# Attention's values in plain float32, a head in each half of the array's columns, one key block for two query blocks

## The chip, the cores and the metric

The kernel runs on one core of one Trainium2 chip. The metric is the device time of one execution in microseconds (us): 2129.85 us before the change, the median of 3 runs (2129.79 to 2129.86).

## The reference

First attention: 4 batches, 8 heads, 768 tokens, head size 64, all in float32. A token sees the 4 first tokens of its sequence (the sinks) and the window of 128 tokens that ends in itself:

```
scores = scale * np.matmul(q, k.transpose(0, 1, 3, 2))
keep = is_sink | in_window            # rel >= 0 and rel < window; sinks: pos < 4
a = np.exp(scores - max) ; a = a / (a.sum(-1) + 1e-9)
attn_out = np.matmul(a, v)            # "the values"
```

The result, as 3072 rows of 512, goes through a mixture of 8 experts: gate logits `x @ w_gate`, eight rounds of row and column normalization over all tokens (Sinkhorn), and for each expert `relu(x @ w1[e]) @ w2[e]`, weighted and summed.

## The kernel before, in words

Tokens come in 24 blocks of 128 (b, i): 4 batches of 6. A *unit* n is a block with one half of the heads (hh, four heads in two pairs pr): 48 units. Each query block needs two key blocks, its own and the one before, and the 4 sinks.

A round n works on several units at once, in an order written out by hand (`early_round` for n below 6, where TensorE's order alone is fixed; `steady_round` from 6 on, where every engine's is). On TensorE (PE), steady round n issues:

- `scores(n+1)`, L463: for each pair of heads three products of the split q and k (float32r: high x high, high x low, low x high). A head's 64 rows lie in one half of the array's rows, and the two heads alternate. Head h writes the PSUM bank st*h*, one buffer each.
- `values(n-1, 0)`, L539: the first pair. V (`split_v`, L455, on POOL) and the probabilities PT (`transpose_p`, L501: ACT copies the high part L514, DVE subtracts for the low part L517) are split likewise. The stationary operand is 128 keys x the 128 columns of *two* heads, the moving one the probabilities of both heads (256 columns), so each product has two useful quarters of four. Two key blocks x three terms, and one matmul of 96 rows for the sinks: seven per pair, L555.
- one step of `run_fill` (expert 0's products, L633 and L649, spread over the rounds), a `gate_step` (L580, one matmul of the gate's logits).
- `transpose_qk(n+2)` into st0: four transposes L439; ACT casts the high part (L445), DVE subtracts the low one (L448).
- `transpose_p(n)`, pair 0 into st1, pair 1 into st2: eight transposes L510 (four where i is 0).
- `values(n-1, 1)`, the second pair, and `store_x(n-1)` (L557): ACT and DVE copy 64 rows each of O into xr (L565); SP stores xr when both halves of the heads are there, and the gate's matmuls of this block are queued for the next round.
- `transpose_sinks(n)` (L535), another gate step, another fill step.

DVE's order in the round is: `soften(n+1)` (L487, mask and minimum; ACT takes the exponentials, L490), copies that were left over, `divide(n+1)` (L496, L497; POOL scales by the reciprocal, L499), the expert fill's low part, then L448, L517 twice, L565. SP's queue loads k, q and v rows (L429) two to four rounds ahead. So `scores` of the next round waits for L448 (st0), for L517 twice (st1, st2) and for ACT's copy of the sinks' transpose (st3).

O and the gate's output share two PSUM buffers; all eight banks are taken. After attention come the Sinkhorn rounds, and experts 1 to 7 and the other two thirds of the tokens, from L904 on, which the diff leaves alone.

Of the kernel before, what the change touches and what calls it, by code (L numbers as in the profile page):

```python
# [9 lines left out]
F32 = mybir.dt.float32  # L10
# [223 lines left out]
def tile_sink_attention_moe(ctx: ExitStack, tc: tile.TileContext, q, k, v, wg, w1, w2, out):  # L234
# [60 lines left out]
    NK = H * SINK  # L295
    SK = 3 * NK
    bd = attc.tile([SK, H], F32, name="bd")
    nc.gpsimd.memset(bd, 1.0)
    for r0 in range(0, SK, NK):
        blk = bd[r0:r0 + NK, :]  # L300
        nc.gpsimd.affine_select(out=blk, in_=blk, pattern=[[-SINK, H]], compare_op=ALU.is_ge, fill=0.0,
                                base=0, channel_multiplier=1)
        last_const = nc.gpsimd.affine_select(out=blk, in_=blk, pattern=[[SINK, H]], compare_op=ALU.is_ge, fill=0.0,
                                             base=SINK - 1, channel_multiplier=-1).ins
# [68 lines left out]
    SS = []  # L373
    for j in range(2):
        s = att1.tile([P, SK], F32R, name=f"SS{j}")
        nc.vector.tensor_copy(s, zero[:, 0:SK])
        SS.append(s)
# [10 lines left out]

    units = [(b, i, hh) for b in range(B) for i in range(NB) for hh in range(2)]
# [5 lines left out]
    VSr, VSm = {}, {}  # L395
# [8 lines left out]
    def load_sinks(b):  # L404
        vs = VSr[b] = att.tile([SK, D], F32, name="vs")
        for r0 in range(0, SK, NK):
            (nc.sync if b else nc.scalar).dma_start(vs[r0:r0 + NK, :], v[b, :, 0:SINK, :])

    def spread_sinks(b):

        vm = VSm[b] = att1.tile([P, H, D], F32, name="vm")[0:SK]
        nc.gpsimd.tensor_tensor(vm, VSr[b].unsqueeze(1).broadcast_to([SK, H, D]), bd.unsqueeze(2).broadcast_to([SK, H, D]), op=ALU.mult)

    def split_sinks(b):

        VS = seq[b] = att.tile([SK, H * D], F32R, name="VS")
        vmf = VSm[b].rearrange("p h d -> p (h d)")
        nc.gpsimd.tensor_scalar(VS, vmf, 1.0, 1.0, op0=ALU.mult, op1=ALU.mult)
        nc.gpsimd.tensor_sub(VS[2 * NK:], vmf[2 * NK:], f32(VS[2 * NK:]))

    def load_rows(names, j):
        b, i = divmod(j, NB)
        cuts = (0, HH, H) if j == 0 else (0, H)
        ts = [(att.tile([P, H, D], F32, name=nm), {"kr": k, "qr": q, "vr": v}[nm]) for nm in names]
# [29 lines left out]

    def split_v(n):  # L455
        b, i, hh = units[n]
        V = att.tile([P, 2, HH * D], F32R, name="V", bufs=5)
        vs = raws["vr", b, i][:, hh * HH:(hh + 1) * HH, :].rearrange("p h d -> p (h d)")
        nc.gpsimd.tensor_scalar(V[:, 0], vs, 1.0, 1.0, op0=ALU.mult, op1=ALU.mult)
        nc.gpsimd.tensor_sub(V[:, 1], vs, f32(V[:, 0]))  # L460
        us[n]["V"] = V
# [38 lines left out]

    def transpose_p(n, pr):  # L501
# [6 lines left out]
        for j, w in enumerate(ws):  # L508
# [4 lines left out]
        PT = u["PT", pr] = att.tile([P, 2, len(ws), 2, P], F32R, name="PT", bufs=4)  # L513
        hi = nc.scalar.copy(PT[:, 0], t).ins  # L514

        def low():
            u["split"] = hi, nc.vector.tensor_sub(PT[:, 1], t, f32(PT[:, 0])).ins  # L517

        return low

    def gather_sinks(n):

        hh = units[n][2]
        ss = SS[hh]
        nk = HH * SINK
        snk = us[n]["sc"][:, :, 0:SINK]
        v3 = lambda c0: ss[:, c0 + hh * nk:c0 + (hh + 1) * nk].rearrange("p (h s) -> p h s", s=SINK)
        for c0 in (0, 2 * NK):
            nc.gpsimd.tensor_scalar(v3(c0), snk, 1.0, 1.0, op0=ALU.mult, op1=ALU.mult)
        nc.gpsimd.tensor_sub(v3(NK), snk, f32(v3(0)))  # L530

    def transpose_sinks(n):

        tsk = st_tile([SK, P], 3)
        nc.tensor.transpose(tsk, f32(SS[units[n][2]]), ident)  # L535
        PS = us[n]["PS"] = att.tile([SK, P], F32R, name="PS")
        nc.scalar.copy(PS, tsk)

    def values(n, pr):  # L539

        b, i, hh = units[n]
        u = us[n]
        if pr == 0:
            u["O"] = ps_o.tile([P, NP, 2, P], F32, name="O")
        cs = slice(pr * P, (pr + 1) * P)
        ops = []
        ws = (1,) if i == 0 else (0, 1)
        for j, w in enumerate(ws):
            V = us[n - 2 + 2 * w]["V"]
            for x_, y_ in ((0, 0), (0, 1), (1, 0)):  # L550
                ops.append((V[:, x_, cs], u["PT", pr][:, y_, j]))
        if i:
            ops.append((seq[b][:, hh * HH * D:][:, cs], u["PS"].unsqueeze(1).broadcast_to([SK, 2, P])))
        for j, (x_, y_) in enumerate(ops):
            nc.tensor.matmul(u["O"][:, pr], lhsT=x_, rhs=y_, start=(j == 0), stop=(j == len(ops) - 1))  # L555

    def store_x(n):  # L557
        b, i, hh = units[n]
        u = us[n]
        O = u["O"]  # L560
        quads = [(slice(r * D, (r + 1) * D), O[r * D:(r + 1) * D, :, r, :]) for r in range(2)]
        tok = b * S + i * P
        xr = u["xr"] = us[n - 1]["xr"] if hh else att.tile([P, KC, P], F32, name="xr")
        for (rows, o), cp_ in zip(quads, (nc.scalar.copy, nc.vector.tensor_copy)):
            cp_(xr[rows, hh * NP:(hh + 1) * NP, :], o)  # L565
        if hh == 1:
            nc.sync.dma_start(xscr[:, :, tok:tok + P].rearrange("k p t -> p k t"), xr)
            if tok < NPART:
                cols = slice(tok % HT, tok % HT + P)
                for kh in range(2):  # L570
                    x_ = xr[:, kh * KH:(kh + 1) * KH, :]
                    b_ = xblock(kh, tok // HT)
                    act_soon(lambda b_=b_, x_=x_: nc.scalar.copy(b_[:, 0, :, cols], x_))
                    pool_soon(lambda b_=b_, x_=x_: nc.gpsimd.tensor_sub(b_[:, 1, :, cols], x_, f32(b_[:, 0, :, cols])))
            later.append(gate_tile(tok // P, xr))
# [166 lines left out]
    def spin(k_, w):  # L742

        for _ in range(k_):
            nc.tensor.matmul(spare[0:SK, 0:w * SK], lhsT=SS[1], rhs=SS[1].unsqueeze(1).broadcast_to([P, w, SK]), start=True, stop=True)

    def early_round(n):

        if units[n + 2][2] == 0:
            with (tc.high_priority() if n == -2 else nullcontext()):  # L750
                load_rows(("kr", "qr"), n // 2 + 1)
                load_rows(("vr",), n // 2 + 1)
            if units[n + 2][1] == 0:
                load_sinks(units[n + 2][0])
        if n == -2:
            nc.sync.dma_start(wg_raw, wg.rearrange("(k p) e -> p k e", p=P))
            spread_sinks(0)
            split_sinks(0)
# [16 lines left out]
        if on(n - 1):  # L775
            values(n - 1, 0)
# [5 lines left out]
        if on(n):  # L782
            transpose_p(n, 0)()
            if units[n][1]:
                gather_sinks(n)
            with tc.issue_after(us[n - 1]["scaled"] if n else last_const):
                split_v(n)
# [3 lines left out]
        if on(n - 1):  # L791
            values(n - 1, 1)
            store_x(n - 1)
# [11 lines left out]
    def steady_round(n):  # L805

        if n % 2 == 0:
            if on(n + 2):
                load_rows(("vr",), n // 2 + 1)
# [13 lines left out]
        if on(n):  # L823
            if units[n][1]:
                gather_sinks(n)
            split_v(n)
# [3 lines left out]
        if on(n - 1):  # L830
            values(n - 1, 0)
# [15 lines left out]
        if on(n - 1):  # L847
            values(n - 1, 1)
# [13 lines left out]
        if on(n):  # L862
            b, i, hh = units[n]
            if (i, hh) == (0, 0):
                spread_sinks(b)
            elif (i, hh) == (0, 1):
                split_sinks(b)
# [785 lines left out]
```

## Time and profile before

| | |
|---|---|
| median of 3 runs | 2129.85 us |
| span of the profiled execution | 2128.0 us, first to last instruction |
| PE busy | 2115.4 us, 99% |
| DVE, ACT, POOL busy | 1521.0, 882.5, 751.2 us |
| attention with its fill | the rounds up to some 287 us |

Of the profiled execution the span alone is given; 1.85 us are between it and the median. Rows of the trace give an instruction's start and duration in us, its engine (PE matmul, PEld weight load, DVE, ACT, POOL, SP's queue SPq), its line, what it writes and reads, partitions x elements and a count of merged neighbours. In brackets stands how long its engine had been idle and what released it. PE's durations run from issue to the end of the result, so neighbours overlap; the distance of their starts is what each costs.

### The profile page before, as it was taken

The numbers are of one execution on the slowest core, as the hardware profiler recorded it, in microseconds if no ns is written. First come the engines' busy times: TensorE is split into PE (matmuls) and PEld (weight loads), VectorE is DVE, ScalarE is ACT, GpSimd is POOL, SyncE is SP. The second block draws the span as 40 slices with busy tenths as digits, with TensorE's granted clock in tenths as the row PEclk, the third lists the DMA queues.
The fourth block names the chain that finished last, engine by engine and source line by source line (L and its number), as shares of the span: only waits on it lengthen the run. The fifth ranks groups of instructions, "written<-read, shape, count | busy, mean of one in ns | idle before, by whom it ended". The sixth has DMA issues, their size and how long they took to land.

```text
span 2128.0 us, 31779 instructions
## 1 busy us (share of the span) xinstructions
PE 2115.4 (99%) x10541; PEld 1767.1 (83%) x10541; DVE 1521.0 (71%) x2722; ACT 882.5 (41%) x1867; POOL 751.2 (35%) x950
## 2 busy tenths in 40 slices
PE   9999999999999999999999999999999999999998
PEld 7898887888888888888888888888888888888887
DVE  8877778778777876866766666666756766666666
ACT  7877745444444443442233322332333232332322
POOL 7766642323233231232222322223322322233223
PEclk9999999999999999999999999999999999999999
DMA  6543428999999887686666666667866666666662
GB/s 146 130 101 86 96 95 271 319 295 312 294 302 305 293 290 241 226 280 199 207 195 201 207 189 207 202 203 277 282 201 192 203 204 198 200 204 195 202 198 85
DMA packets 397642, 453.83 MB, mean 213 GB/s; under 512 B 99680, under 2 KB 265760, under 8 KB 396576
## 3 DMA queue, kind: packets, MB, share of 16 engines
q1 hardware_dynamic: 397080, 451.57, 68.0%
q8 instruction: 87, 1.43, 0.3%
q14 instruction: 83, 0.68, 0.1%
q10 hardware_dynamic: 392, 0.16, 0.0%
HBM read 314.17 MB, written 137.46 MB: 212 GB/s over the span
## 4 chain that ended last, share of the span: by engine, by line
PE 95%; DVE 2%; ACT 2%; issue 0%; POOL 0%; DMA 0%; SPq 0%; DVEq 0%; POOLq 0%; ACTq 0%
PE c L916 41%; PE o L1477 20%; PE held L1477 8%; PE o L1160 7%; PE held L1160 7%; PE O L555 3%; PE st L479 2%; PE st L510 1%; PE o L649 1%; ACT sc L490 1%; PE g L633 1%; PE st L439 1%; PE st L633 0%; PE O L580 0%; DVE PT L517 0%; PE O L649 0%
## 5 line engine op out<-in xcount | busy, mean ns | idle before, releaser
L942 ACT CAST hf<-w 128x512 fp32r<-128x512 f32 x448 | 265.2, 620 | 563.9 <-POOL w L1442 299.7
L1477 PE MATMUL o<-hf,W2q 128*128 128x512 f32 x1920 | 472.0, 389 | 0.0
L1477 PEld LDWEIGHTS o<-hf,W2q 128*128 128x128 f32 x1920 | 360.1, 188 | 75.4 <-DVE acc L1491 0.9
L916 PE MATMUL c<-T,W1q 128*128 128x512 f32 x1530 | 388.9, 389 | 0.2 <-DVE w L1423 0.2
L943 DVE TENSOR_TENSOR hf<-w,hf 128x512 fp32r<-128x512 f32 x448 | 330.5, 766 | 74.8 <-ACT hf L942 67.3
L916 PEld LDWEIGHTS c<-T,W1q 128*128 128x128 f32 x1530 | 286.9, 188 | 60.6 <-DVE w L1423 0.9
L1491 DVE TENSOR_TENSOR acc<-o,acc 128x512 f32<-128x512 f32 x298 | 204.6, 687 | 170.2 <-PE o L1477 170.2
L916 PE MATMUL c<-B,W1q 128*128 128x512 f32 x1134 | 278.3, 389 | 0.0
L1442 POOL TENSOR_TENSOR w<-w 128x512 f32<-128x512 f32 x64 | 82.7, 1292 | 492.4 <-DVE w L1424 486.2
L916 PEld LDWEIGHTS c<-B,W1q 128*128 128x128 f32 x1134 | 212.6, 188 | 43.9
L1423 DVE TENSOR_TENSOR w<-c,M 128x512 f32<-128x512 f32 x192 | 132.3, 689 | 137.5 <-PE c L916 133.1
L1419 ACT COPY M<-c 128x512 f32<-128x512 f32 x192 | 112.7, 587 | 247.7 <-PE c L916 247.6
L1477 PE MATMUL held<-hf,W2q 128*128 128x512 f32 x768 | 194.8, 389 | 0.0
L916 PE MATMUL c<-T,W1f 128*128 128x512 f32 x672 | 171.1, 390 | 0.1
L1160 PE MATMUL held<-W2f,h 128*128 128x512 f32 x672 | 171.1, 390 | 0.0
L1160 PE MATMUL o<-W2f,h 128*128 128x512 f32 x672 | 170.6, 389 | 0.1
L1477 PEld LDWEIGHTS held<-hf,W2q 128*128 128x128 f32 x768 | 144.0, 188 | 29.8
L1459 POOL TENSOR_TENSOR w<-w 128x512 f32<-128x512 f32 x64 | 105.6, 1651 | 176.2 <-DVE hf L943 176.2
L1160 PEld LDWEIGHTS o<-W2f,h 128*128 128x128 f32 x672 | 126.0, 188 | 27.0 <-DVE acc L1167 0.9
L916 PEld LDWEIGHTS c<-T,W1f 128*128 128x128 f32 x672 | 125.8, 188 | 26.9 <-issue 0.5
L1160 PEld LDWEIGHTS held<-W2f,h 128*128 128x128 f32 x672 | 125.8, 188 | 26.4 <-DVE W2f L943 0.5
L969 POOL TENSOR_TENSOR r<-r 128x256 f32<-128x256 f32 x27 | 20.1, 743 | 357.7 <-ACT M L1123 221.2
(212 smaller groups left out, 3088.5 us busy)
## 6 DMA issues: line engine op xcount, KB each, us to landing
W2q<-w2s SPq DMA_DIRECT2D x448, 256.0 KB, 3.0
W1q<-w1s SPq DMA_DIRECT2D x444, 256.0 KB, 2.9
w1s<-W1f SPq DMA_DIRECT2D x56, 896.0 KB, 7.8
w2s<-WT SPq DMA_DIRECT2D x136, 256.0 KB, 3.5
r<-in_moe_w_dram SPq DMA_DIRECT2D x64, 512.0 KB, 4.4
w2s<-W2f SPq DMA_DIRECT2D x56, 256.0 KB, 4.7
PB<-psd SPq DMA_DIRECT2D x16, 512.0 KB, 4.2
w2s<-W2f SPq DMA_DIRECT2D x56, 128.0 KB, 6.5
```

The source lines that it names most:

```text
L479: nc.tensor.matmul(ps[h], lhsT=Q[r0:r0 + D, a, pr, :], rhs=K[r0:r0 + D, c, pr, :], start=(j == 0), stop=(j == 2))
L555: nc.tensor.matmul(u["O"][:, pr], lhsT=x_, rhs=y_, start=(j == 0), stop=(j == len(ops) - 1))
L916: nc.tensor.matmul(ps, lhsT=w1(a, k), rhs=x[:, b, k, :], start=(start and j == 0), stop=(stop and j == len(TERMS) - 1), skip_group_check=n ...
L942: nc.scalar.copy(dst[:, 0], src)
L943: at(1, lambda: nc.vector.tensor_sub(dst[:, 1], src, f32(dst[:, 0])))
L1160: nc.tensor.matmul(o, lhsT=h[c, th][:, a, off:off + P], rhs=W2F[n][:, w, c, :], start=(begin and c == 0 and j == 0), stop=(end and c == 1 ...
L1419: nc.scalar.copy(t, T["c2"])
L1423: nc.vector.tensor_add(w, T["c1"], T[m])
L1442: nc.gpsimd.tensor_sub(S3, T["A11"], T["A21"])
L1459: at(k, lambda: nc.gpsimd.tensor_sub(T["A11"], w, T["A11"]))
L1477: nc.tensor.matmul(o, lhsT=W2Q[part, n, m][:, a, k * P:(k + 1) * P], rhs=F[part, n, H_OF[m]][:, w, :], start=(j == 0 and (begin or not hol ...
L1491: nc.vector.tensor_add(sums[m, k], o, sums[m, k])
```

## The change

The values use V and the probabilities as they are, in plain float32. The stationary operand is one head's 64 columns of V, and its output the half of PSUM's partitions that belongs to it, so two heads sit in the two halves of the array's columns. A key block meets both query blocks that need it (its own and the next) in one matmul of 256 columns, once the next block's probabilities are there: a block's result is begun in one unit (ACT's copy to xr) and completed two units later (DVE adds), and then stored and gated. A few blocks finish at once (`whole`: blocks 1 and 3 of the first batch and the last one); blocks 2 and 4 of the first batch begin with one query. The sinks' matmul is one per head, 128 columns, with operands padded with zeros to 128 rows. `values` of both pairs now stand together behind the scores. Probabilities are kept in a ring of three places per key block; the splits of V, of the probabilities and of the sinks go. The scores, the experts and the rest are unchanged. The diff, cut to its core:

```diff
-        vm = VSm[b] = att1.tile([P, H, D], F32, name="vm")[0:SK]
-        nc.gpsimd.tensor_tensor(vm, VSr[b]..., bd..., op=ALU.mult)
-    def split_sinks(b): ...
+VSs = [att1.tile([P, 2, HH, D], F32, name=f"VS{j}") for j in range(2)]
+PSs = [att1.tile([P, P], F32, name=f"PS{j}") for j in range(4)]
+for t in VSs + PSs:
+    nc.gpsimd.memset(t, 0.0)
+    def spread_sinks(b, hh):
+        nc.gpsimd.tensor_tensor(seq[b][0:NK, hh], VSr[b][:, hh]..., bd..., op=ALU.mult)
 ...
-    def split_v(n):
-        nc.gpsimd.tensor_scalar(V[:, 0], vs, 1.0, 1.0, op0=ALU.mult, op1=ALU.mult)
-        nc.gpsimd.tensor_sub(V[:, 1], vs, f32(V[:, 0]))
 ...
+    RING = 3
+    spot = lambda n, s: (2 * block(n) + s) % RING
     def transpose_p(n, pr):
-        ws = (1,) if i == 0 else (0, 1)
+        ws = sorted([(spot(n, 0), 1)] + ([(spot(n - 2, 1), 0)] if i else []))
         t = st_tile([P, len(ws), 2, P], (2 if n < 2 else 1) + pr)
 ...
-        hi = nc.scalar.copy(PT[:, 0], t).ins
         def low():
-            u["split"] = hi, nc.vector.tensor_sub(PT[:, 1], t, f32(PT[:, 0])).ins
+            u["split"] = nc.vector.tensor_copy(PT, t).ins,
 ...
+    def due_keys(n):
+        whole = (b, i) in ((0, 1), (0, 3)) or n >= L - 2
+        if i == 0:
+            return ([(n - 2, {n - 2: 0})], [n - 2], []) if b else ([], [], [])
+        if (b, i) in ((0, 2), (0, 4)):
+            return [(n - 2, {n: 1})], [], [n]
+        return [(n - 2, {n - 2: 0, n: 1})] + ([(n, {n: 0})] if whole else []), [n - 2, n] if whole else [n - 2], [] if whole else [n]
 
     def values(n, pr):
-            for x_, y_ in ((0, 0), (0, 1), (1, 0)):
-                ops.append((V[:, x_, cs], u["PT", pr][:, y_, j]))
-            ops.append((seq[b][:, hh * HH * D:][:, cs], u["PS"].unsqueeze(1).broadcast_to([SK, 2, P])))
-            nc.tensor.matmul(u["O"][:, pr], lhsT=x_, rhs=y_, start=(j == 0), stop=(j == len(ops) - 1))
+        for m, qs in keys:
+            R = spots(PTR[hh][pr], [spot(m, s_) for s_ in qs.values()])
+            for h in range(2):
+                ops.append((h, raws[("vr", *units[m][:2])][:, hh * HH + 2 * pr + h, :], R[:, h], ...))
+        for q_ in ready:
+            if units[q_][1]:
+                for h in range(2):
+                    ops.append((h, seq[units[q_][0]][:, hh, 2 * pr + h, :], us[q_]["PS"].unsqueeze(1), ...))
+        for j, (h, x_, y_, sides) in enumerate(ops):
+            nc.tensor.matmul(u["O"][h * D:(h + 1) * D, pr, sides], lhsT=x_, rhs=y_, start=(j < 2), stop=(j >= len(ops) - 2))
 
     def store_x(n):
-        for (rows, o), cp_ in zip(quads, (nc.scalar.copy, nc.vector.tensor_copy)):
-            cp_(xr[rows, hh * NP:(hh + 1) * NP, :], o)
+        for q_ in sorted(begun + ready, key=...):
+            if "begun" in us[q_]:
+                nc.vector.tensor_add(xr[:, half, :], O, xr[:, half, :])
+            else:
+                nc.scalar.copy(xrs[block(q_)][:, half, :], O)
+        if hh == 1:
+            for q_ in ready:
+                put_x(q_)        # the store, the pieces for the experts, the gate: as before
 ...
     def steady_round(n):
-            if on(n + 2):
-                load_rows(("vr",), n // 2 + 1)
+            if on(n):
+                load_rows(("vr",), n // 2)
 ...
         if on(n - 1):
-            values(n - 1, 0)
+            for pr in range(NP):
+                values(n - 1, pr)
         run_fill(1)
 ...
         if on(n - 1):
-            values(n - 1, 1)
             store_x(n - 1)
```

The early rounds have the values together at the first place, too. The sinks of a unit are now gathered with one POOL copy instead of three operations, and their transpose has 16 columns instead of 96.

## Rows read from the trace of the kernel before

**Rows 1.** The page of the profiled execution: its span; the engines' busy time, share and instructions; PE's busy tenths and granted clock in 40 equal slices; the chain that ended last, by engine.

```profile
span 2128.0 us, 31779 instructions
...
PE 2115.4 (99%) x10541; PEld 1767.1 (83%) x10541; DVE 1521.0 (71%) x2722; ACT 882.5 (41%) x1867; POOL 751.2 (35%) x950
...
PE   9999999999999999999999999999999999999998
...
PEclk9999999999999999999999999999999999999999
...
PE 95%; DVE 2%; ACT 2%; issue 0%; POOL 0%; DMA 0%; SPq 0%; DVEq 0%; POOLq 0%; ACTq 0%
```

**Rows 2.** Busy time of each engine by stretch: us from the span's start, then the length, then busy us and instructions of PE, PEld, DVE, ACT, POOL, the granted clock, DMA share and GB/s.

```profile
34.00:287.00 253.00, 251.57 (x2176) 227.93 (x2177) 197.19 (x663) 195.98 (x608) 168.15 (x392) 1.00 0.41 96
...
340.00:2128.00 1788.00, 1780.66 (x7878) 1471.70 (x7876) 1252.13 (x1864) 642.61 (x1146) 536.09 (x464) 1.00 0.73 232
```

**Rows 3.** PE's instructions in order of time, one round (start us, duration us, engine, line, op, out<-in, stationary rows*columns, moving rows x columns, count); the first row is the start of the scores two rounds earlier.

```profile
192.74 0.98 PE L479 MATMUL st<-KQ 64*128 64x260 f32 x12
...
204.65 0.99 PE L479 MATMUL st<-KQ 64*128 64x260 f32 x12
205.56 0.98 PE L555 MATMUL O<-PT,V 128*128 128x256 f32 x6
206.38 0.28 PE L555 MATMUL O<-PS,VS 96*128 96x256 f32 x1
206.50 0.88 PE L633 MATMUL g<-B,W 128*128 128x256 f32 x6
207.22 0.28 PE L580 MATMUL O<-wg_raw,xr 128*128 128x8 f32 x2
207.35 0.31 PE L439 MATMUL st<-ident,kr 128*128 128x128 f32 x1
...
207.82 1.04 PE L510 MATMUL st<-ident,sc 128*128 128x128 f32 x8
208.62 0.96 PE L555 MATMUL O<-PT,V 128*128 128x256 f32 x6
209.41 0.28 PE L555 MATMUL O<-PS,VS 96*128 96x256 f32 x1
209.53 0.27 PE L535 MATMUL st<-ident,SS 128*96 128x128 f32 x1
209.56 0.93 PE L649 MATMUL o<-W1f,h 128*128 128x512 f32 x3
210.43 0.39 PE L479 MATMUL st<-KQ 64*128 64x260 f32 x2
```

**Rows 4.** All engines in order of time, 201.4 to 204.9 us, from the last q/k transposes to the next scores.

```profile
201.71 0.60 PE L510 MATMUL st<-ident,sc 128*128 128x128 f32 x4
...
201.91 0.58 ACT L445 CAST KQ<-st 128x512 fp32r<-128x512 f32 x1
...
202.52 0.69 DVE L448 TENSOR_TENSOR KQ<-st,KQ 128x512 fp32r<-128x512 f32 x1 [0.24 <-ACT KQ L445]
...
203.13 1.28 DVE L517 TENSOR_TENSOR PT<-st,PT 128x512 fp32r<-128x512 f32 x2
...
204.64 0.42 PEld L479 LDWEIGHTS st<-KQ 64*128 64x128 f32 x6 [0.36 <-DVE PT L517]
```

**Rows 5.** Who waited for whom, 40 to 280 us, PE's weight loads: us in total, times, the longest.

```profile
PEld st L479 <- DVE PT L517: 11.6, 33, 0.4
PEld st L479 <- ACT xr L565: 2.7, 6, 0.8
```

**Rows 6.** PE in order of time around a transpose with one output column (L34).

```profile
291.97 0.86 PE L649 MATMUL o<-W2f,h 128*128 128x512 f32 x3
292.67 0.27 PE L34 MATMUL st<-ident,m 128*1 128x128 f32 x1
292.69 0.48 PE L633 MATMUL st<-B,W 128*128 128x256 f32 x2
```

**Rows 7.** The listing of one line: the only DVE copy of 128x512 out of PSUM (durations in ns: least, median, most; first and last start in us).

```profile
L1561 DVE COPY w<-held x1: 692/692/692, 2120.7 to 2120.7; 128x512 f32<-128x512 f32 x1
```

**Rows 8.** Groups of instructions by line and shape, 40 to 280 us (busy us, mean ns of one | idle before, releaser).

```profile
L517 DVE TENSOR_TENSOR PT<-st,PT 128x512 fp32r<-128x512 f32 x72 | 46.1, 681 | 0.2
...
L514 ACT CAST PT<-st 128x512 fp32r<-128x512 f32 x70 | 38.8, 587 | 0.6 <-ACT PT L514 0.3
...
L460 POOL TENSOR_TENSOR V<-vr,V 128x256 fp32r<-128x256 f32 x41 | 30.2, 736 | 3.4
...
L565 DVE COPY xr<-O 64x256 f32<-64x256 f32 x42 | 18.0, 428 | 1.3
```

**Rows 9.** The chain that ended last, early rounds (start us, us, what).

```profile
28.42 1.20 DVE PT L517 x2
29.65 0.43 DVE xr L565
```

**Rows 10.** POOL in order of time at the start: a memset and the first division.

```profile
0.94 0.32 POOL L276 MEMSET mask<- 128x260 f32 x1
...
11.08 1.86 POOL L499 TENSOR_SCALAR sc<-sc,st 128x260 f32<-128x260 f32 x4 [0.59 <-ACT sc L490]
```

**Rows 11.** DMA issues between 40 and 280 us, the loads of V (count, KB each, median us to landing).

```profile
vr<-in_v_dram SPq DMA_DIRECT2D x19, 256.0 KB, 3.0
```

More of the change, by code (lines that the diff above doesn't have):

```diff
@@ L293, in tile_sink_attention_moe @@
     nc.vector.memset(zero, 0.0)
-    NK = H * SINK
-    SK = 3 * NK
-    bd = attc.tile([SK, H], F32, name="bd")
+    NK = HH * SINK
+    bd = attc.tile([NK, HH], F32, name="bd")
     nc.gpsimd.memset(bd, 1.0)
[L299 to L304, printed above, removed]
+    nc.gpsimd.affine_select(out=bd, in_=bd, pattern=[[-SINK, HH]], compare_op=ALU.is_ge, fill=0.0,
+                            base=0, channel_multiplier=1)
+    last_const = nc.gpsimd.affine_select(out=bd, in_=bd, pattern=[[SINK, HH]], compare_op=ALU.is_ge, fill=0.0,
+                                         base=SINK - 1, channel_multiplier=-1).ins
     wg_raw = attc.tile([P, KC, E], F32, name="wg_raw")
@@ L371, in tile_sink_attention_moe @@
     att = ab.enter_context(tc.tile_pool(name="att", bufs=2))
[L373 to L377, printed above, removed]
+    ZC = 96
+    none = att1.tile([P, ZC], F32R, name="none")
+    nc.vector.tensor_copy(none, zero[:, 0:ZC])
     KQ = []
@@ L404, in load_sinks @@
     def load_sinks(b):
[L405 to L409, printed above, removed]
-        vm = VSm[b] = att1.tile([P, H, D], F32, name="vm")[0:SK]
[L412 to L419, printed above, removed]
+        vs = VSr[b] = att.tile([NK, 2, D], F32, name="vs")
+        for hh in range(2):
+            (nc.sync if b else nc.scalar).dma_start(vs[:, hh, :], v[b, hh * HH:(hh + 1) * HH, 0:SINK, :])
+    def spread_sinks(b, hh):
+        seq[b] = VSs[b % 2]
+        nc.gpsimd.tensor_tensor(seq[b][0:NK, hh], VSr[b][:, hh].unsqueeze(1).broadcast_to([NK, HH, D]), bd.unsqueeze(2).broadcast_to([NK, HH, D]), op=ALU.mult)
     def load_rows(names, j):
@@ L423, in load_rows @@
         cuts = (0, HH, H) if j == 0 else (0, H)
-        ts = [(att.tile([P, H, D], F32, name=nm), {"kr": k, "qr": q, "vr": v}[nm]) for nm in names]
+        ts = [(att.tile([P, H, D], F32, name=nm, bufs=3 if nm == "vr" else 2), {"kr": k, "qr": q, "vr": v}[nm]) for nm in names]
         for (t, _), nm in zip(ts, names):
@@ L499, in divide, with spots @@
             u["scaled"] = nc.gpsimd.tensor_scalar(sc[:, h, :], sc[:, h, :], rs[:, h:h + 1], 1.0, op0=ALU.mult, op1=ALU.mult).ins
+    RING = 3
+    PTR = [[att1.tile([P, 2, RING, P], F32, name=f"PT{hh}{pr}") for pr in range(NP)] for hh in range(2)]
+    block = lambda n: units[n][0] * NB + units[n][1]
+    spot = lambda n, s: (2 * block(n) + s) % RING
+    def spots(held, where):
+        at_ = sorted(where)
+        return held[:, :, at_[0]:at_[-1] + 1:max(at_[-1] - at_[0], 1)]
     def transpose_p(n, pr):
@@ L505, in transpose_p @@
         sc = u["sc"]
-        ws = (1,) if i == 0 else (0, 1)
+        ws = sorted([(spot(n, 0), 1)] + ([(spot(n - 2, 1), 0)] if i else []))
         t = st_tile([P, len(ws), 2, P], (2 if n < 2 else 1) + pr)
-        for j, w in enumerate(ws):
+        for j, (_, w) in enumerate(ws):
             for h in range(2):
@@ L542, in values @@
         u = us[n]
+        keys, ready, _ = due_keys(n)
+        if not keys:
+            return
         if pr == 0:
             u["O"] = ps_o.tile([P, NP, 2, P], F32, name="O")
-        cs = slice(pr * P, (pr + 1) * P)
+            u["side"] = {q_: j for j, q_ in enumerate(sorted(keys[0][1], key=lambda q_: spot(keys[0][0], keys[0][1][q_])))}
         ops = []
-        ws = (1,) if i == 0 else (0, 1)
-        for j, w in enumerate(ws):
-            V = us[n - 2 + 2 * w]["V"]
-            for x_, y_ in ((0, 0), (0, 1), (1, 0)):
-                ops.append((V[:, x_, cs], u["PT", pr][:, y_, j]))
@@ L552, in values @@
-        if i:
-            ops.append((seq[b][:, hh * HH * D:][:, cs], u["PS"].unsqueeze(1).broadcast_to([SK, 2, P])))
-        for j, (x_, y_) in enumerate(ops):
-            nc.tensor.matmul(u["O"][:, pr], lhsT=x_, rhs=y_, start=(j == 0), stop=(j == len(ops) - 1))
-    def store_x(n):
+        for m, qs in keys:
+            R = spots(PTR[hh][pr], [spot(m, s_) for s_ in qs.values()])
+            sides = sorted(u["side"][q_] for q_ in qs)
+            for h in range(2):
+                ops.append((h, raws[("vr", *units[m][:2])][:, hh * HH + 2 * pr + h, :], R[:, h], slice(sides[0], sides[-1] + 1)))
@@ new lines, in values @@
+        for q_ in ready:
+            if units[q_][1]:
+                for h in range(2):
+                    ops.append((h, seq[units[q_][0]][:, hh, 2 * pr + h, :], us[q_]["PS"].unsqueeze(1), slice(u["side"][q_], u["side"][q_] + 1)))
+        for j, (h, x_, y_, sides) in enumerate(ops):
+            nc.tensor.matmul(u["O"][h * D:(h + 1) * D, pr, sides], lhsT=x_, rhs=y_, start=(j < 2), stop=(j >= len(ops) - 2))
+    xrs = {}
+    def store_x(n):
+        hh = units[n][2]
+        u = us[n]
+        _, ready, begun = due_keys(n)
+        half = slice(hh * NP, (hh + 1) * NP)
+        for q_ in sorted(begun + ready, key=lambda q_: (q_ in ready, q_)):
+            O = u["O"][:, :, u["side"][q_], :]
+            if "begun" in us[q_]:
+                xr = xrs[block(q_)]
+                nc.vector.tensor_add(xr[:, half, :], O, xr[:, half, :])
+            else:
+                if hh == 0:
+                    xrs[block(q_)] = att.tile([P, KC, P], F32, name="xr", bufs=3)
+                nc.scalar.copy(xrs[block(q_)][:, half, :], O)
+                us[q_]["begun"] = True
+        if hh == 1:
+            for q_ in ready:
+                put_x(q_)
@@ L558, in store_x, with put_x @@
+    def put_x(n):
         b, i, hh = units[n]
-        u = us[n]
-        O = u["O"]
-        quads = [(slice(r * D, (r + 1) * D), O[r * D:(r + 1) * D, :, r, :]) for r in range(2)]
         tok = b * S + i * P
-        xr = u["xr"] = us[n - 1]["xr"] if hh else att.tile([P, KC, P], F32, name="xr")
-        for (rows, o), cp_ in zip(quads, (nc.scalar.copy, nc.vector.tensor_copy)):
-            cp_(xr[rows, hh * NP:(hh + 1) * NP, :], o)
[L566 to L575, printed above, removed]
+        xr = xrs.pop(block(n))
+        nc.sync.dma_start(xscr[:, :, tok:tok + P].rearrange("k p t -> p k t"), xr)
+        if tok < NPART:
+            cols = slice(tok % HT, tok % HT + P)
+            for kh in range(2):
+                x_ = xr[:, kh * KH:(kh + 1) * KH, :]
+                b_ = xblock(kh, tok // HT)
+                act_soon(lambda b_=b_, x_=x_: nc.scalar.copy(b_[:, 0, :, cols], x_))
+                pool_soon(lambda b_=b_, x_=x_: nc.gpsimd.tensor_sub(b_[:, 1, :, cols], x_, f32(b_[:, 0, :, cols])))
+        later.append(gate_tile(tok // P, xr))
@@ L744, in spin @@
         for _ in range(k_):
-            nc.tensor.matmul(spare[0:SK, 0:w * SK], lhsT=SS[1], rhs=SS[1].unsqueeze(1).broadcast_to([P, w, SK]), start=True, stop=True)
+            nc.tensor.matmul(spare[0:ZC, 0:w * ZC], lhsT=none, rhs=none.unsqueeze(1).broadcast_to([P, w, ZC]), start=True, stop=True)
     def early_round(n):
@@ L785, in early_round @@
                 gather_sinks(n)
-            with tc.issue_after(us[n - 1]["scaled"] if n else last_const):
-                split_v(n)
         gate_step()
@@ L822, in steady_round @@
                 scores(n + 1, pr)
[L823 to L826, printed above, removed]
+        if on(n) and units[n][1]:
+            gather_sinks(n)
         if on(n + 1):
@@ L830, in steady_round @@
         if on(n - 1):
-            values(n - 1, 0)
+            for pr in range(NP):
+                values(n - 1, pr)
         run_fill(1)
```

43 lines of the change are left out of this document (17 added, 26 removed).

## The prediction

> **What bounds the kernel now.** First the page: TensorE is busy 99% of the span, its clock is granted in full in every slice, and the chain that ended last is 95% PE [rows 1]. That alone doesn't say which stage the change touches, so next the busy times by stretch: attention with its early expert work fills 34 to 287 us; from 340 us on there is expert work alone, which the diff leaves as it is [rows 2]. Only the first part can gain or lose, some 40 steady rounds, and there PE is the busiest engine with the others well below.
>
> So I read one round on PE in order of time [rows 3]; what counts is from one group's start to the next, since the durations shown overlap. From 204.65: scores 0.91 us, first half of the values 0.94 (seven matmuls of 256 columns), half a fill step 0.72, a gate step 0.13, the four q/k transposes 0.47, eight probability transposes 0.80, second half of the values 0.91, sink transpose and fill 0.90, next scores at 210.43. The round is 5.78; the two since 192.74 took 11.91 [rows 3], so the other kind is 6.13, and the mean 5.95.
>
> Three things stand in these rows. Twelve score matmuls of 260 columns in 0.91 us are faster than seven of 256 in 0.94: two heads run at once in the halves of the array's rows. Entering and leaving that mode costs: at 0.12 for a matmul of 256 columns (0.72 for the fill's six) the seven behind the scores would take 0.83 and not 0.94, the six pairs of scores 0.71 and not 0.91, and the fill ahead of them, three of 512 columns at 0.23 [rows 6], 0.69 and not 0.87 (0.08 of that is the transpose before it, which shows too short). That is 0.11 + 0.20 + 0.10 for two changes of mode, some 0.21 each. Third, PE's loads stood idle 0.36 us ahead of the scores, released by DVE's L517 [rows 4], 33 times between 40 and 280 us, 11.6 us in all [rows 5]. Today that wait lies almost wholly under the change of mode. It is the nearest other bound.
>
> **What that wait is made of.** The scores of h1 and h2 reuse the PSUM banks st1 and st2 out of which L517 copies. From the end of the q/k transposes (201.71, where the next transposes start) ACT casts KQ from 201.91, DVE subtracts from 202.52 (L448), L517 follows twice from 203.13 and ends at 204.41 [rows 4]: 2.70 us. With 0.1 for the weight load that a wait lays bare (an estimate: the transposes, each with a load of its own, follow at 0.11 [rows 3]), 2.80. On PE the way from there to the second pair of scores (0.46 after the first) is 210.43 - 207.82 + 0.46 = 3.07 in one kind of round [rows 3], and 204.65 - 201.71 + 0.46 = 3.40 in the other [rows 3, 4]. So today PE arrives 0.3 to 0.6 late, and DVE has slack.
>
> **The change, part by part.** *The values' own time.* A plain float32 matmul is two records (the gate's, L580 x2 [rows 3]). No row shows a plain matmul of many columns other than a transpose. Lower bound of a record: 0.12 per 256 columns, as now. Upper: a float32 transpose of 128 columns every 0.11 us (twelve in 1.27 [rows 3]), so 0.22 per 256. I take 0.22, the row of the same type; but its loads come at the same pace, so it may be the load that it shows. A full round then has 8 records of 0.22 (one key block, two queries, four heads) and 8 of 0.11 (sinks): 2.64 one after another. If the column halves overlap as the row halves of the scores do, the best is 1.32. But the order is head 0's two records, then head 1's two, and the score pairs start in program order: only the second record of one head meets the first of the other. Laid out so, a pair of heads ends at 0.88, the next starts at 0.77, and both take 1.65.
>
> The Trainium skill (TensorE: Matmul & The Clock Gate, Part 3) says that matmuls never overtake each other, and that column tiles overlap, 2.38 times for three; the rows agree for row halves, none shows columns. With free order the values would cost 1.32 instead of 1.65.
>
> *Changes of mode.* Full, row, full becomes full, row, column, full: one more. Bounds: 0.21 by the scores, and 0 by the transpose with one output column at 292.67, which starts where the 512 columns before it end and delays nothing [rows 6]. I take 0.21, since a plain matmul is nearer to the scores' than to a transpose. Values: 1.65 + 0.21 = 1.86, against 1.85 today.
>
> The Trainium skill (TensorEngine Tiling (Array Packing), Key Properties) says that a change of mode drains the engine, a change of tile within one doesn't. The scores' 0.21 agrees; by the transpose's row the stage would be some 7 us shorter (0.21 in the 33 rounds where nothing else takes it up).
>
> *Both halves of the values move ahead of the transposes.* This is what I expect to decide. PE's way from the q/k transposes to the second score pair loses 0.92: 2.15 and 2.48 remain. The way over ACT and DVE stays 2.80: ACT's cast of KQ and L448 are untouched, and L517 turns from a subtraction of 128x512 (0.68 [rows 8]) into a copy out of PSUM, of which the one other row takes 0.69 [rows 7]. ACT's two casts of PT at 0.59 vanish, but L517 follows L448 without a gap [rows 4], so it didn't wait for them. PE thus waits 0.65 or 0.32, mean 0.48, where it waited for nothing. Queued behind the waiting scores is all of PE's next round, and DVE's L487 and ACT's exponentials wait for the scores in turn.
>
> *Sum over the 40 rounds 6 to 45.* 23 full rounds: values +0, wait +0.5: +11. Six with a batch's first block (no second query: 16 records of 0.11, staggered, give 1.0 + 0.21 for 0.90): +0.3 and a wait of 0.3: +4. Six with its second block (no sinks, 1.08 + 0.21 for 1.85): -0.55, wait +0.5: 0. Three with one query and no sinks: values -1.1, wait +1: 0. Two where a block finishes both keys (2.7 for 1.85, wait 0.4): +2.5. Sum +17. Rounds 46 to 48, where the last block finishes at once, and two tiles' gates together: +2.
>
> *Early rounds.* Up to 34 us one DVE/ACT chain sets the time, and DVE's 0.43 copy of xr lies on it [rows 9]; in rounds 3 to 6 it goes to ACT (a first contribution is copied there): -2. The first two blocks finish together, so four POOL subtractions come at once in round 4, and again in round 8: 0 to +1, I take 0.
>
> *Free.* V's splits on POOL (the subtraction alone 0.74 a unit) and ACT's PT casts (1.2 a unit) go [rows 8]: both engines are below 80% in the stage [rows 2], and PE's loads wait for ACT 2.7 us of 240 [rows 5]. xr: ACT copies 128x256 instead of 64x256, DVE adds 128x256 instead of copying 64x256 (0.43 [rows 8]), behind L517 as now. POOL's new memsets (1536 columns; 260 take 0.32 [rows 10], so 1.9 us) replace two V splits and the sinks' splits, covered until the first division at 11.1 us [rows 10]; without that cover, 1.9 once. SP: V's load is issued two rounds later, ahead of the k and q loads as before; landing takes 3.0 us [rows 11], and its reader comes one to three rounds (5.8 us or more) later. Stores and gates of x move two rounds back; the fill that reads block 5 starts in round 17, and block 5 ends in 14.
>
> Together 17 + 2 - 2 = +17 on the profiled span of 2128.0, which lies 1.85 under the median of the runs, 2129.85 (taken as what lies around it). I round down, since the switch was taken at its upper bound: **2146 us**, with a range of its own of 2136 (no switch cost: -7; a chain 0.2 shorter: -8, not both in full) to 2152.
>
> **The rivals.** *The halves don't run at once* (the change doesn't do what it says): values 2.64 + 0.21 a full round, +1 each, and the wait stays, since it doesn't depend on the values: +50, 2180. For it: no row shows column halves. Against: the score pairs show row halves.
>
> *Full overlap and no switch cost*: 1.32. From second score pair to second score pair a round is then 0.46 + 1.32 + 0.72 + 0.13 + 0.47 + 2.80 = 5.90 against a mean of 5.95: no change, 2130. This is also the threshold: a full round gains only under 1.36 for the values.
>
> *DVE's way doesn't bind* (the faster side): if the 2.80 came under 2.15, through a copy much shorter than 0.69 or one that starts ahead of L448, PE's own sum would decide: -3 with the switch, -12 without, -2 early, +2 late: 2118 to 2127, say 2122. For it: ACT and POOL get emptier. Against: L448 and L517 run back to back on DVE.
>
> *A plain record streams at 0.12 per 256 columns*: values near 1.0 with the switch, a round 0.35 shorter in spite of the wait: 2116. Against: the transposes' pace.
>
> **How the numbers follow.** Forecast 0.45; halves in turn 0.20; full overlap 0.15; DVE not binding 0.12; cheap records 0.08. A measurement here tells 0.2% (4.3 us) from no change. Faster 0.12 + 0.08 = 0.20; same 0.15; slower 0.45 + 0.20 = 0.65. The range 2120 to 2182 leaves out the cheap records and the outer edges of the rivals.
>
> **What would show it.** Right: values groups of 1.6 to 1.9 us behind the scores, record starts of the two heads a few ns apart; PE waiting 0.3 to 0.6 a round at the scores for DVE's PT; rounds of 6.4. Wrong: records strictly one after another (2.6); no wait for PT; rounds under 5.9; anything changed after 340 us.

## The result and the profile after

The changed kernel takes 2145.55 us (median of 4 runs, 2143.58 to 2146.69) against 2129.82 us: a ratio of 1.0073, 95% interval 1.0061 to 1.0085, so it is slower by 0.7%. The forecast was 2146.0. Its four executions differ more than the four before (2129.78 to 2129.86), and their mean granted clock goes from 0.998 in the shortest to 0.996 in the longest. The profiled execution has a span of 2143.6 us, 15.6 more than before's; its own run took 2145.38.

By stage, each from the first scores of one round to the first scores of another (us; worked out from the starts of the scores' rows; e1 to e7 are the experiments below):

| | to round 6 | rounds 6-9 | rounds 10-45 | from 46 on | span |
|---|---|---|---|---|---|
| before | 40.9 | 23.8 | 209.7 | 1853.6 | 2128.0 |
| after | 42.7 | 30.1 | 215.1 | 1855.6 | 2143.6 |
| after - before | +1.9 | +6.3 | +5.4 | +2.0 | +15.6 |
| forecast | -2 | +17 for both | | +2 | +17 |
| e1 | 40.8 | 25.4 | 224.9 | 1856.9 | 2147.9 |
| e2 | 43.9 | 26.0 | 200.1 | 1855.9 | 2125.9 |
| e3 | 39.3 | 27.6 | 214.8 | 1856.2 | 2137.7 |
| e4 | 43.9 | 25.2 | 215.0 | 1856.2 | 2140.3 |
| e5 | 45.2 | 31.2 | 216.2 | 1858.2 | 2150.7 |
| e6 | 42.7 | 26.0 | 210.6 | 1855.9 | 2135.2 |
| e7 | 38.9 | 24.3 | 200.2 | 1855.6 | 2118.8 |

So the total was met, but by terms that are not the forecast's. The page of the changed kernel, against [rows 1]:

```profile
span 2143.6 us, 31644 instructions
...
PE 2124.5 (99%) x10669; PEld 1747.0 (82%) x10669; DVE 1506.5 (70%) x2707; ACT 840.2 (39%) x1771; POOL 673.6 (31%) x772
...
PE 97%; DVE 1%; ACT 1%; DMA 1%; issue 0%; POOL 0%; SPq 0%; DVEq 0%; ACTq 0%
```

The other engines did get emptier, and PE, whose share is 99% as before, still took longer: a page in which one engine is nearly full doesn't show that time is being lost. The stretches show a part of it (start and end, length, then busy us of PE, PEld, DVE, ACT, POOL, granted clock, DMA share, GB/s), against [rows 2]:

```profile
34.00:287.00 253.00, 248.28 (x2175) 198.89 (x2172) 178.60 (x635) 155.41 (x514) 103.29 (x229) 0.99 0.40 101
```

PE lost 3.3 us of its 251.57, at a granted clock of 0.99 for 1.00. A steady round on PE in order of time, the same kind as in [rows 3]:

```profile
203.71 1.29 PE L464 MATMUL st<-KQ 64*128 64x260 f32 x12
204.94 0.65 PE L558 MATMUL O<-PT,vr 128*64 128x256 f32 x4
205.42 0.39 PE L558 MATMUL O<-PS,VS 128*64 128x128 f32 x4
205.64 0.60 PE L558 MATMUL O<-PT,vr 128*64 128x256 f32 x4
206.07 0.39 PE L558 MATMUL O<-PS,VS 128*64 128x128 f32 x4
206.39 0.98 PE L651 MATMUL g<-B,W 128*128 128x256 f32 x6
207.20 0.28 PE L598 MATMUL O<-wg_raw,xr 128*128 128x8 f32 x2
...
207.81 1.04 PE L505 MATMUL st<-ident,sc 128*128 128x128 f32 x8
208.69 0.27 PE L523 MATMUL st<-ident,ss 128*16 128x128 f32 x1
208.71 0.95 PE L667 MATMUL o<-W2f,h 128*128 128x512 f32 x3
209.59 0.77 PE L464 MATMUL st<-KQ 64*128 64x260 f32 x3
...
211.13 0.65 PE L558 MATMUL O<-PT,vr 128*64 128x256 f32 x4
```

Group by group, from start to start: scores 1.22 for 0.91 (1.54 in the next round, 209.59 to 211.13), values 1.45 (204.94 to 206.39) for 0.94 + 0.91, fill 0.81 for 0.72, probability transposes 0.87 for 0.80. The round is 5.88 for 5.78, the other kind 6.51 for 6.13: +0.24 on average.

What the scores wait for stands in the rows of all engines ahead of them, against [rows 4]:

```profile
201.62 0.60 PE L505 MATMUL st<-ident,sc 128*128 128x128 f32 x4
...
201.82 0.59 ACT L438 CAST KQ<-st 128x512 fp32r<-128x512 f32 x1 [0.82 <-PE st L432]
...
202.44 0.69 DVE L441 TENSOR_TENSOR KQ<-st,KQ 128x512 fp32r<-128x512 f32 x1 [1.03 <-ACT KQ L438]
...
203.05 1.28 DVE L511 COPY PT<-st 128x512 f32<-128x512 f32 x2
...
204.24 0.41 DVE L571 TENSOR_TENSOR xr<-O,xr 128x256 f32<-128x256 f32 x1
204.38 0.41 PEld L464 LDWEIGHTS st<-KQ 64*128 64x128 f32 x6 [0.18 <-DVE PT L511]
```

The chain from the q/k transposes to the second pair of scores is 201.62 to 204.38, 2.76 us (forecast 2.80): cast, subtraction, two copies, each starting where the one before it ends. PE came there 0.47 us a round too early. The waits of PE's weight loads, 40 to 280 us, answer to [rows 5]:

```profile
PEld st L464 <- DVE PT L511: 8.9, 47, 0.2
```

Read this row with care: it has *less* idle time for L511 than the 11.6 us of [rows 5], though the wait has become real. Before, the loads' idle time lay under the change of mode and cost PE nothing (in e2 below the loads wait 0.2 us in all for the copy that is left to DVE, and the scores take 0.92, as good as the 0.91 before); now the scores themselves start late. The first head of the first pair starts at 203.71, the second only 70 ns later; and much of the wait isn't booked to L511 at all. The distance between the starts of PE's groups is the measure. The copies themselves, against [rows 7, 8] (busy us, mean ns | idle before):

```profile
L511 DVE COPY PT<-st 128x512 f32<-128x512 f32 x66 | 42.3, 680 | 1.4 <-PE st L505 1.3
...
L575 ACT COPY xr<-O 128x256 f32<-128x256 f32 x39 | 14.1, 380 | 4.6 <-DVE xr L571 4.6
...
L571 DVE TENSOR_TENSOR xr<-O,xr 128x256 f32<-128x256 f32 x29 | 11.9, 411 | 0.0
```

A plain copy of 128x512 costs DVE what the subtraction cost (680 for 681 ns), so DVE's part of the chain is as long as before, although the change removed every split of PT.

### The profile page after: what moved, and what is told of

Same layout as the page of the kernel before. It is cut to its first block, busy times and chain, and to the rows that moved or that the text cites. A ratio compares the mean times of both kernels' runs of the same rounds, so it can differ in the third digit from the quotient of the medians.

```text
span 2143.6 us, 31644 instructions
## 1 busy us (share of the span) xinstructions
PE 2124.5 (99%) x10669; PEld 1747.0 (82%) x10669; DVE 1506.5 (70%) x2707; ACT 840.2 (39%) x1771; POOL 673.6 (31%) x772
## 4 chain that ended last, share of the span: by engine, by line
PE 97%; DVE 1%; ACT 1%; DMA 1%; issue 0%; POOL 0%; SPq 0%; DVEq 0%; ACTq 0%
PE c L931 40%; PE o L1492 20%; PE held L1492 8%; PE held L1175 7%; PE o L1175 7%; PE O L558 3%; PE st L464 3%; PE g L651 2%; PE st L505 2%; PE o L667 2%; PE st L432 1%; PE O L598 1%; PE st L651 0%; PE O L667 0%; DVE KQ L441 0%; PE o L763 0%
## 5 line engine op out<-in xcount | busy, mean ns | idle before, releaser
L484 POOL TENSOR_SCALAR sc<-sc,st 128x260 f32<-128x260 f32 x192 | 89.2, 483 | 162.5 <-DVE st L482 117.3
```

Source lines behind the costliest of these rows:

```text
L484: u["scaled"] = nc.gpsimd.tensor_scalar(sc[:, h, :], sc[:, h, :], rs[:, h:h + 1], 1.0, op0=ALU.mult, op1=ALU.mult).ins
```

## Two costs outside the steady rounds

**The early rounds.** Up to round 6 the forecast was -2 and the result +1.9. Busy times of 14 to 19 and 19 to 26 us, first before, then after:

```profile
14.00:19.00 5.00, 4.36 (x35) 3.43 (x35) 3.80 (x16) 3.88 (x13) 4.51 (x11) 1.00 1.05 310
19.00:26.00 7.00, 6.67 (x52) 5.32 (x51) 6.43 (x23) 6.16 (x19) 6.56 (x17) 1.00 0.76 164
```

```profile
14.00:19.00 5.00, 2.41 (x14) 1.41 (x12) 2.94 (x13) 3.42 (x11) 1.53 (x4) 1.00 1.06 366
19.00:26.00 7.00, 5.50 (x28) 4.91 (x29) 4.47 (x15) 4.03 (x13) 2.05 (x5) 0.51 0.31 68
```

All engines do less, PE stands idle for 3.60 us (to 20.41), and from 19 us on its clock is granted at 0.51 (1.2 of 2.4 GHz). ACT and PE of the changed kernel in order of time say for what:

```profile
15.58 1.14 ACT L340 CAST W<-r 128x512 fp32r<-128x512 f32 x2 [3.29 <-DMA r<-in_moe_w_dram]
16.63 0.51 ACT L475 ACTIVATE sc<-sc,st 128x260 f32<-128x260 f32 x1
```

```profile
20.41 1.67 PE L464 MATMUL st<-KQ 64*128 64x260 f32 x12 [3.60 <-DVE KQ L444]
```

ACT waits 3.29 us for a DMA of expert 0's weights, with the exponentials of unit 2 queued behind that cast: they start at 16.63, in e3 below, which undoes this alone, at 14.38, and in the kernel before at 14.68, with the cast behind them at 17.93. The diff made this in a place that doesn't look like a scheduling edit: the casts (`load_plain`) are issued after the instructions in `us[...]["split"]`. That tuple held ACT's cast of PT *and* DVE's subtraction; now it holds DVE's copy alone. With no instruction of ACT in it, nothing keeps the cast behind ACT's work, and it went ahead of the next unit's exponentials.

**Rounds 7 and 8.** The block that finishes at once has a copy (ACT) and an addition (DVE) to issue, and `store_x` issues the addition's block first. One ACT row, one PE row, one POOL row and another PE row of the changed kernel, in order of time:

```profile
63.88 0.37 ACT L575 COPY xr<-O 128x256 f32<-128x256 f32 x1 [2.28 <-DVE xr L571]
```

```profile
64.45 0.62 PE L464 MATMUL st<-KQ 64*128 64x260 f32 x5 [0.50 <-ACT PS L525]
```

```profile
65.05 3.25 POOL L592 TENSOR_TENSOR B<-xr,B 128x256 fp32r<-128x256 f32 x4 [2.73 <-ACT B L591]
```

```profile
67.21 0.80 PE g L651 x2
...
68.23 0.95 PE st L432 x4
```

(The last two are from the chain that ended last.) ACT's copy comes out 2.28 us late, its queue holds the sinks' copy PS for which the scores wait, then the experts' pieces; POOL's four subtractions of those pieces start later for it, and the fill waits for them. From 67 to 74 us the clock is granted at 0.51 again: four q/k transposes take 0.95 us of the chain, 0.22 from start to start where they have 0.11 at the full clock. Round 9 takes 10.28 us for 6.11.

## The experiments

**e1: the old values, together.** Only the place of the second half is changed, in the kernel before:

```diff
 def steady_round(n):      # the kernel before
             values(n - 1, 0)
+            values(n - 1, 1)
 ...
-            values(n - 1, 1)
             store_x(n - 1)
```

> The kernel before with one edit: in the steady rounds the second half of the values stands right behind the first, ahead of the transposes; everything is still split float32r. Theory (the wait for DVE's copies of the probabilities, whose way from the q/k transposes to the second pair of scores keeps its 2.8 us while PE's way loses 0.9): 0.3 to 0.65 us of wait in each of some 38 rounds, scores groups of 1.2 to 1.5 us where they took 0.91, 2144 to 2150. Rival (the loss of the change lies in the plain products, the column mode and the early rounds): 2129 to 2131, no new wait.

2148.77 us, ratio 1.0086 (1.0073 to 1.01). PE in order of time:

```profile
203.31 1.27 PE L479 MATMUL st<-KQ 64*128 64x260 f32 x12
204.51 0.98 PE L555 MATMUL O<-PT,V 128*128 128x256 f32 x6
...
209.39 0.38 PE L479 MATMUL st<-KQ 64*128 64x260 f32 x1
```

As the theory had it: the scores take 1.20 for 0.91 without a single new instruction, and the rounds are 6.08 and 6.76. The order by itself costs more than the whole change.

**e2: ACT copies one of the two PT.** In the changed kernel, steady rounds:

```diff
+        if steady[0] and pr == 0:
+            u["split"] = nc.scalar.copy(PT, t).ins,
+            return lambda: None
```

> The changed kernel with one edit: in the steady rounds ACT instead of DVE copies the first pair's probabilities, right behind its cast of KQ, so that DVE has one copy of 0.6 less between the q/k transposes and the scores. Theory (that way is what the rounds wait for): scores groups back to 0.9 to 1.0 us, rounds of 5.55 and 5.9, some 0.45 us less in 36 rounds, 2127 to 2132. Rival (the rounds are as long as PE's own work makes them): 2144 to 2147.

2126.94 us, ratio 0.9986 (0.9977 to 0.9995), just below the theory's 2127 to 2132: 18.6 us under the changed kernel and a little under the kernel before. 15 of the 18.6 are gained in rounds 10 to 45, and 4.1 in rounds 6 to 9, where this kernel's clock stays full from 67 to 74 us. ACT and DVE, then the two next groups on PE:

```profile
190.13 0.58 ACT L511 COPY PT<-st 128x512 f32<-128x512 f32 x1
190.26 0.69 DVE L441 TENSOR_TENSOR KQ<-st,KQ 128x512 fp32r<-128x512 f32 x1 [0.87 <-ACT KQ L438]
...
190.87 0.68 DVE L515 COPY PT<-st 128x512 f32<-128x512 f32 x1
```

```profile
191.53 0.99 PE L464 MATMUL st<-KQ 64*128 64x260 f32 x12
192.45 0.65 PE L562 MATMUL O<-PT,vr 128*64 128x256 f32 x4
```

The first copy runs beside L441 instead of behind it, the scores are back at 0.92, and rounds are 5.58 and 5.91: 0.30 and 0.60 under the changed kernel, the size of the wait, and 0.21 under the kernel before, which is what the new values are worth by themselves.

**e3: the casts held back.** In `load_plain` the changed kernel's casts wait for the next unit's exponentials, too (`us[n]["exp"]` is the last of them, on ACT):

```diff
-                for ins in us[1 + 2 * u + j]["split"]:
+                for ins in (*us[1 + 2 * u + j]["split"], us[2 + 2 * u + j]["exp"]):
```

> The changed kernel with one edit in the early rounds alone: the first expert's weight casts on ACT are held back behind the exponentials of the following unit, as they were in effect before. Theory (ACT's queue stood 3.3 us at those casts, waiting for the weights' load, ahead of the exponentials; TensorE then fell to half clock at 19.2 us): rounds 1 and 2 fall from 7.4 and 6.3 us to about 5 each, no half clock before 30 us, 2139 to 2143. Rival (the early rounds are longer because PE has too little work there without the first values): no change, 2144 to 2147.

2139.51 us, ratio 1.0046 (1.0032 to 1.006): 6.0 less, the theory's size. Busy times of 19 to 26 us:

```profile
19.00:26.00 7.00, 6.09 (x60) 4.62 (x58) 5.76 (x22) 5.13 (x18) 2.91 (x7) 1.00 0.32 73
```

The clock stays at 1.00 there. Of the 5.9 us of span, 3.5 are gained up to round 6 and 2.6 in rounds 6 to 9, of which the theory said nothing: this kernel's clock stays full there as well, rounds 7 and 8 take what the changed kernel's take (6.94 and 7.65 for 6.94 and 7.64), and round 9 takes 7.65 for 10.28. These 2.6 us are the price of the second stretch at half clock.

**e4: copies first.** In `store_x`, the block that begins goes ahead of the one that is ready:

```diff
-        for q_ in sorted(begun + ready, key=lambda q_: (q_ in ready, q_)):
+        for q_ in sorted(begun + ready, key=lambda q_: ("begun" in us[q_], q_)):
```

> The changed kernel with one edit: where a block is completed and another finishes in the same unit, ACT's first copy is issued ahead of DVE's addition instead of behind it. Theory (in rounds 7 and 8 ACT's queue stands 2.3 us at that copy, and the sinks' copy, the next scores and the fill's pieces are queued behind it, until TensorE falls to half clock): round 8 and 9 lose 3 to 5 us of their 7.6 and 10.3, 2140 to 2143. Rival (the four subtractions on POOL that come at once are the cause): round 9 stays near 10, 2144 to 2147.

2141.26 us, ratio 1.0052 (1.0038 to 1.0066): 4.3 less, the theory's size again. Rounds 6 to 9 take 4.9 us less, though three of the four subtractions on POOL still come in a row; the early rounds show 1.2 more, as much as e2's, which doesn't touch them, so differences of that size between executions are not to be explained.

**e5: head by head.** In the changed kernel, all matmuls of a pair's first head are issued ahead of the second's (start and stop follow):

```diff
+        ops = [o for h_ in range(2) for o in ops if o[0] == h_]
```

> The changed kernel with one edit: within each pair of heads, all matmuls of the values of the first head are issued before all of the second, instead of in turn. The work is the same. Theory (two column halves overlap only as far as neighbours in program order lie in different halves): a full round's values go from 1.25 us (both heads' records 6 to 7 ns apart) towards 2.5, less the one record of each pair that still meets the other half; the wait for DVE's copies stays, since it ends before the values start. About 23 full rounds at +1.0 and 12 smaller ones at half of that: +28 to +35, 2173 to 2181 us. Rival (the order doesn't matter, the two halves run side by side however they are issued): 2144 to 2148.

2151.35 us, ratio 1.0097 (1.0082 to 1.0112). Neither: my theory's 2173 to 2181 falls, since rounds 10 to 45 cost 1.0 us more in all, and so does the rival, since the time isn't the same. PE of e5 in a round where a head has eight records in a pair, which shows why:

```profile
60.69 0.86 PE L560 MATMUL O<-PT,vr 128*64 128x256 f32 x4
61.39 0.27 PE L560 MATMUL O<-PS,VS 128*64 128x128 f32 x1
61.39 0.43 PE L560 MATMUL O<-PT,vr 128*64 128x256 f32 x1
61.49 0.38 PE L560 MATMUL O<-PS,VS 128*64 128x128 f32 x2
```

The first head's four PT records start alone, and the second head's first PT record starts with the first head's first PS record (61.39), ahead of three PS records that stand before it in program order. This group takes 3.35 us for 2.32. In a steady round a head has only four records in a pair; there the second head starts 13 ns after the first, and the group takes 1.50 for 1.45. So a matmul of the other half passed three records in both cases, and not the seven that it stands behind here.

**e6: the second pair of values back.** In the changed kernel, steady rounds:

```diff
-            for pr in range(NP):
-                values(n - 1, pr)
+            values(n - 1, 0)
 ...
+            values(n - 1, 1)
             store_x(n - 1)
```

> The changed kernel with one edit: in the steady rounds the second pair of heads' values goes back behind the probability transposes, where the kernel before had its second half; the first pair stays behind the scores. Theory (the 0.47 us that PE waits at the scores comes from the place of the values, and every separate group of values pays its own change of mode): PE's way to the second score pair is some 0.7 us longer and the wait goes, 0.47 in some 36 rounds, -17; a second entry into the column mode and exit from it cost 0.2 to 0.4 in each, +7 to +14: 2136 to 2144 us, scores groups of 0.9 again. Rival (the scores group is longer for another reason, the new form of the copy): the wait stays and the modes are added, 2152 to 2160.

2138.06 us, ratio 1.0037 (1.0024 to 1.0051), inside the theory's range; 4.5 us are gained in rounds 10 to 45 and 4.2 in rounds 6 to 9, where the clock stays full here, too. PE, one round:

```profile
202.70 0.98 PE L464 MATMUL st<-KQ 64*128 64x260 f32 x12
203.61 0.65 PE L558 MATMUL O<-PT,vr 128*64 128x256 f32 x4
...
206.98 0.65 PE L558 MATMUL O<-PT,vr 128*64 128x256 f32 x4
...
208.92 0.99 PE L464 MATMUL st<-KQ 64*128 64x260 f32 x12
```

The scores take 0.91 again; the rounds are 5.82 and 6.23, 0.17 less on average. With 0.47 saved, the second entry and exit of the column mode cost 0.30 a round (0.15 of it inside the values, 0.80 + 0.80 for 1.45).

**e7: e2, e3 and e4 together.**

> The changed kernel with three edits together: in steady rounds ACT copies the first pair's PT (-18.6 alone), the first expert's weight casts are held behind the next unit's exponentials as in the kernel before (-6.0 alone), and ACT's copy of a block that begins goes ahead of DVE's addition to one that is ready (-4.3 alone). If the three costs are separate, in different rounds, as the theory has them: 2145.5 - 18.6 - 6.0 - 4.3 = 2116.6, so 2115 to 2119 us, faster than the kernel before by 0.5 to 0.7%. Rival (they share the same idle time, above all the stretch after the early rounds): 2121 to 2126.

2122.41 us, ratio 0.9964 (0.9951 to 0.9978): faster than both kernels, by the rival's number. The theory counted one thing three times. e2, e3 and e4 each gain in rounds 6 to 9 (4.1, 2.6 and 4.9; table), and together they gain 5.9 of these 11.6. In each of the three alone the clock stays full from 67 to 74 us, so each saving should have the 2.6 us of that stretch (e3) in it. Counted three times instead of once, they are 5.2 of the 5.8 us by which the sum missed; what the rest is, no run shows. Busy times of e7 there:

```profile
67.00:74.00 7.00, 7.00 (x65) 5.56 (x63) 5.09 (x16) 5.21 (x17) 3.90 (x9) 1.00 0.34 100
```

## Why the prediction was right, and where it was wrong

**The deciding step was right in mechanism and size**: both halves of the values ahead of the transposes shorten PE's way, and the way over ACT and DVE binds. Forecast 0.65 and 0.32, mean 0.48; measured 0.63 and 0.31, mean 0.47. e1 shows that the order alone makes it, e2 that shortening DVE's chain takes it away. Of the signs named ahead, heads a few ns apart and the wait for PT came; values groups of 1.6 to 1.9 us (1.45) and rounds of 6.4 (6.19 on average) did not.

**"Laid out so, both take 1.65" failed.** In the trace the records of the two heads start 6 to 7 ns apart, from the first one on. In the rows of values above, 205.64 to 206.07 are two such pairs of 256 columns, 205.42 to 205.64 two of 128: 0.216 and 0.109 a pair. Four of each are 1.30 for a full round, the 1.32 of the rival with full overlap, not 1.65. The reason given, that starts follow program order, is refuted by e5's rows. The Trainium skill (TensorE: Matmul & The Clock Gate, Part 3) says that matmuls start strictly in the order of the program; here they don't when they lie in different halves of the columns, and the measurement decides. The Trainium skill (TensorEngine Tiling (Array Packing), Key Properties) has tiles operating independently, with which the rows agree.

**The price of a record was right, and that of the mode nearly.** A record takes 0.216 per 256 columns where 0.22 was taken from the transposes, and the column mode adds 0.25 to the values and the fill (0.05 at its start, 0.10 at its end, 0.10 in the fill behind it) where 0.21 was taken. 0.11 of the old values' 1.85 was the price of leaving the row mode, by the prediction's own working; so against the two changes of mode before, the third costs some 0.14. The rival with no such cost is refuted, by e6's 0.30 as well. So in a full round values and mode give a net -0.22 instead of 0, and +0.24 in all instead of +0.5.

**Not every round is the full one.** Rounds 10 to 45 lost 5.4 us where the forecast had about 14.5 of its 17 (the other 2.5 is the two blocks that finish at once). By kind (from the starts of the scores): the 23 full rounds lost 7.3, forecast 11; the six with a batch's first block lost 2.1, forecast 4; the six with its second block gained 3.7, forecast 0; the one with one query gained 0.4. In three of the second-block rounds (15, 27 and 39) the scores took 1.75 us in the kernel before already, so a wait was there before the change that one round, read as a pattern, doesn't show.

**The early rounds' -2, from DVE's copy of xr going to ACT, was missed.** The step looked at what the copy costs and not at who else read `us["split"]`: the diff's one-element tuple let ACT's casts of the weights ahead of the exponentials, and the forecast was missed by 3.9 (+1.9 for -2). With the queue's order mended, the time up to round 6 is 39.3 (e3) and 38.9 (e7) against 40.9, the forecast's size; but that the copy gives it is not shown, and the match may be luck. Rounds 3 and 4, where the copy moved, take 10.9 us together before and in e7, and 1.7 of e7's 2.0 lie in round 5 (5.27 for 6.96), whose block has one query and no sinks now.

**"0 to +1, I take 0" for the POOL subtractions that come at once left a wait out.** Rounds 6 to 9 lost 6.3 us where the two blocks that finish at once were to cost 2.5. The subtractions come late as well as together, since ACT's queue stands behind DVE's addition, and a stretch at half clock follows; with ACT's copy first (e4) these rounds lose 1.4.

**These errors cancelled**: some 9.1 us too much in rounds 10 to 45, some 7.7 too little in front of them (3.9 up to round 6, 3.8 in rounds 6 to 9). The 2145.55 is therefore less of a confirmation than it looks. The rival in which DVE's way doesn't bind had 2122 us; e7, which makes that condition true and mends the rest, is at 2122.4, though the values gain more in it than that rival had, and rounds 46 on cost its +2.

What stays open: why the clock fell at 67 us in the changed kernel and not in e2 or e3, whose waits just before are nearly the same. No run here separates that, and only one execution of each kernel has a trace: by the granted clocks of the changed kernel's four executions, how much of the time is at half clock may differ from one to the next.

## What to carry to other kernels

When work is moved past a point where one engine hands over to another, count the way over both engines from the same starting point; here 0.92 us of PE's work covered a chain of ACT and DVE that no list of busy times shows, and sharing the chain between ACT and DVE gained more (e2) than the change had lost. Look for everything that reads a name whose content the diff changes: an ordering hint that loses an engine's instruction moves other work in that engine's queue. Savings measured alone add up only if they lie in different stretches; compare them stage by stage before summing.

## What was not expected of the hardware

Plain float32 matmuls in the two halves of the array's columns run side by side at once: two records of 256 columns in 0.216 us, 6 to 7 ns apart, even when the program has one head's matmuls behind the other's; a record passed three that stand before it, not seven. A DVE copy of 128x512 out of PSUM takes as long as a subtraction of that size (680 and 681 ns). And after waits of PE the granted clock stood at 0.51 twice in one execution (19 to 26 and 67 to 74 us), in which the transposes stood 0.22 us apart for 0.11. Rounds 6 to 9 of e3, whose waits there are nearly the same but whose clock stayed full, are 2.6 us shorter.
